# A fused attention and gated-FFN layer: one Strassen product for the down projections of chunks 0 and 1

## The chip, the cores and the metric

One core of a Trainium2 chip (trn2) runs one kernel launch. The metric is device time in microseconds (us), the time of that core. The kernel before took 777.2 us as the median of 3 runs (776.82 to 777.21).

## What is computed

Two layers in a row on 2048 positions of width 1024, in bf16: a pre-norm attention with a dilated window of 8 keys, and a pre-norm feed-forward part in which gate and up are multiplied without an activation.

```python
qkv = layernorm(x) @ wqkv                       # D = 1024, 32 heads of 32
logits[s, w] = q[s] . k[s - 2*w] * 32**-0.5     # w = 0..7, -1e9 where s - 2*w < 0
o = softmax(logits) @ v[s - 2*w]
h = x + o @ wo
n = layernorm(h)
out = h + ((n @ w_gate) * (n @ w_up)) @ w_down  # F = 3584
```

## The kernel before

The 2048 positions are worked in four chunks of 512 (TC). The width lies in eight blocks of 128 (KO), the hidden width F in 28 blocks of 128 (NF), or 14 pairs of blocks (NP). `tc.manual_schedule()` means that every engine runs its instructions in the order in which the Python code records them; nothing reorders them later.

Stages, in the order of TensorE:

- Query, key and value of all chunks (`qkv`, matmuls in `mm_group`, L409). ScalarE copies each result out of PSUM (L324) and SyncE's queue writes it to DRAM; GpSimd's queue reads it back in the layout of the attention (`load_qk`, `load_v`).
- Attention (`attention`, L444) runs on VectorE alone. It is a generator. First come the logits (L451 to L461), then the softmax, then eight weighted value products and their sums (L494, L499, L502, L504). At its end GpSimd's queue writes `oD` to DRAM (`od`, L506) and reads it back transposed as `oT`, in four parts (L509).
- The output projection of chunks 0 and 1 with the second layernorm (`wo_ln2`, L519): 64 matmuls (L532) in eight groups, VectorE's add of the residual (L534), the statistics (L181), the root on ScalarE (L185, L186), the normalised rows on VectorE (L190), and four transposing DMAs on SyncE's queue (L526), which together give `lnT`.
- Gate and up of chunks 0 and 1 (`ffn1`, L602): 448 matmuls a chunk, ScalarE copies (L611, L616), VectorE's product (L617), with ScalarE's sums of absolute values (`Scale.add`, L560) for the scales of the fp16 stages.
- The down projection of chunk 0 (`ffn2`, L640): 224 matmuls (L646), four results at a time. It stands between `wo_ln2(1)` and `ffn1(1)` (L777 to L825).
- The down projection of chunk 1 by Strassen's scheme within the chunk: its rows are split in two halves of 256 and its hidden blocks in even and odd ones. Seven products (`dprod`, L805) of 28 matmuls each take the place of 224. The operands are sums and differences in fp16, made by VectorE (L800, L929, L954, L958, L988); scaled copies come from ScalarE (L786) and VectorE (L788). The output projections of chunks 2 and 3 (`wo_adds`, L846; L934 and L969) stand between these products.
- Gate, up and down of chunks 2 and 3 together, by Strassen's scheme over both chunks (`pair_block`, L703, and `dprod`).

The order of VectorE's work around the change comes from `Background` (L37). Foreground code calls `bg.step(us)` after a group of matmuls; this adds that many microseconds (times `rate`) to a credit, and while the credit is positive the next step of a waiting generator, as a rule the attention, is recorded. `bg.spend(us)` takes VectorE's foreground work off the credit. `bg.finish(g)` records all that is left of a generator at that place. Thus the place of each attention operation in VectorE's list is fixed when the code is built.

Weights come through one list, `stream` (L130 to L156); `pump` (L161) issues the next load on SyncE's queue while fewer than seven tiles of `wstream` are in use, and `retire` (L173) gives tiles back. PSUM has eight banks, all under one tag.

Of the kernel before, what the change touches and what calls it, by code (L numbers as in the profile page):

```python
# [8 lines left out]
BF = mybir.dt.bfloat16  # L9
# [69 lines left out]
def kernel(  # L79
# [41 lines left out]

    bg = Background()
# [13 lines left out]
    def stream_wd(c, hf):  # L136
        for b in range(4):
            stream.append((("wd", c, hf, b), wd_v[:, bass.ts(b, 7), bass.ts(hf, 512)], 7))

    NH = NF // 4  # L140
    for c in range(2):
        stream_wo(c)
        if c > 0:
            stream_wd(0, 0)
            stream_wd(0, 1)
        for b in range(7):
            stream.append((("wg", c, b), wg_v[:, :, bass.ts(b, 512)], KO))
            stream.append((("wu", c, b), wu_v[:, :, bass.ts(b, 512)], KO))
    def stream_down(name, e, hf, halves):
        for a in halves:  # L150
            stream.append((("dn", name, a), wd_e[e][:, bass.ts(a, 7), bass.ts(hf, 512)], 7))

    stream_down("21", 1, 0, (0, 1))
    stream_down("11", 0, 0, (0, 1))
    stream_wo(2)
    stream_down("12", 0, 1, (0,))  # L156
# [286 lines left out]

    def attention(c):  # L444
        qD, kD = qkv_in["q", c], qkv_in["k", c]
        lg = att.tile([128, W, SUB], F32, tag="lg", name=f"lg{c}")
        for wp in range(W // 2):
# [14 lines left out]
            yield 1.0  # L462
        if c == 0:
            nc.vector.tensor_tensor(lg[0:32, :, 0:16], lg[0:32, :, 0:16], mask[:], ALU.add)
# [54 lines left out]
    def wo_ln2(c):  # L519
# [8 lines left out]
        for t in range(4):  # L528
            for hf in range(2):
# [5 lines left out]
                if hf == 1:  # L535
                    stats(hs[t], mv4, t)
                    rstd_of(mv4, rs4, t, t + 1)
                    bg.spend(1.5)
                elif t > 0:
                    norm(t - 1)  # L540
                    bg.spend(0.55)
                bg.spend(0.7)
                bg.step(GROUP_US)
# [38 lines left out]
    scale_gu, scale_d, scale_h = Scale("gu", 56), Scale("d", 56), Scale("h", 56)  # L582
    scale_h1 = Scale("h1", 28)

    def abs_sum(c, b, j):
        wt = wts["wg" if c == 0 else "wu", c, b]
        junk = lnp.tile([128, 2, 512], BF, tag="ln", name=f"junk{c}_{b}_{j}")
        scale_gu.add(28 * c + 4 * b + j, wt[:, bass.ts(j, 2), :], junk[:])

    def abs_sum_down(hf, b, j):  # L590
        junk = lnp.tile([128, 512], BF, tag="ln", name=f"junkd{hf}_{b}_{j}")
        scale_d.add(28 * hf + 7 * b + j, wts["wd", 0, hf, b][:, j, :], junk[:])
# [5 lines left out]
    def abs_sum_h1(f, ht):  # L598
        junk = lnp.tile([128, TC], BF, tag="ln", name=f"junke{f}")
        scale_h1.add(f, ht[:], junk[:])  # L600

    def ffn1(c, lnT, at={}):  # L602
        hT = []
        for b in range(7):
            if b == 5 and c + 1 < NCH:
                hss[c + 1] = load_x(c + 1, "h", nc.sync)
            for j in range(4):
                pg = psum.tile([128, TC], F32, tag="mm", name=f"pg{c}_{b}_{j}")
                mm_group(pg, wts["wg", c, b], j, lnT)
                gs = t1k.tile([128, TC], BF, tag="t1k", name=f"gs{c}_{b}_{j}")  # L610
                nc.scalar.copy(gs[:], pg[:])  # L611
                bg.step(GROUP_US)
                pu = psum.tile([128, TC], F32, tag="mm", name=f"pu{c}_{b}_{j}")
                mm_group(pu, wts["wu", c, b], j, lnT)
                us = t1k.tile([128, TC], BF, tag="t1k", name=f"us{c}_{b}_{j}")
                nc.scalar.copy(us[:], pu[:])  # L616
                nc.vector.tensor_tensor(gs[:], gs[:], us[:], ALU.mult)  # L617
                abs_sum(c, b, j)
                bg.spend(0.45)
                bg.step(GROUP_US)  # L620
                hT.append(gs)
                if (b, j) in at:
                    at[b, j]()
                f = len(hT) - 3
                if c == 1 and f >= 0:
                    abs_sum_h1(f, hT[f])
            retire(2)
            if b in at:
                at[b]()
        if c == 1:  # L630
            for f in range(NF - 2, NF):
                abs_sum_h1(f, hT[f])
        return hT

    def ffn2_store(c, t, hf, acc, hs, lo=0, n=512):
        cols = bass.ds(hf * 512 + lo, n)
        nc.vector.tensor_tensor(hs[t][:, cols], acc[:], hs[t][:, cols], ALU.add)
        nc.sync.dma_start(outf[bass.ds(c * TC + t * 128, 128), cols], hs[t][:, cols])

    def ffn2(c, hf, hT, hs, between={}):  # L640
        acc = [psum.tile([128, 512], F32, tag="mm", name=f"acc{c}_{hf}_{t}") for t in range(4)]
        for b in range(4):
            for j in range(7):
                f = b * 7 + j
                for t in range(4):
                    nc.tensor.matmul(acc[t][:], lhsT=hT[f][:, bass.ts(t, 128)],  # L646
                                     rhs=wts["wd", c, hf, b][:, j, :],
                                     start=(f == 0), stop=(f == NF - 1))
                if c == 0:
                    abs_sum_down(hf, b, j)  # L650
                bg.step(0.86)
            retire()
            if b in between:
                between[b]()
        for t in range(4):
            ffn2_store(c, t, hf, acc[t], hs)
            bg.spend(0.7)


# [104 lines left out]
    pump(pair_at)  # L764
    qkv(2, range(6))
    start_attention(2)
    hss[0] = load_x(0, "h", nc.sync)
    qkv(3, range(4), last=True)
    bg.finish(atts[0])
# [4 lines left out]
    lnT2, hs = nxt  # L774
    hT = ffn1(0, lnT2)
    bg.finish(atts[1])
    nxt = wo_ln2(1)  # L777
    for hf in range(2):
        ffn2(0, hf, hT, hs)
    lnT2, hs = nxt  # L780
# [37 lines left out]
    dn = {}  # L818

    def first_blocks():  # L820
        dn["11"] = [wts["dn", "11", a] for a in range(2)]
        dn["21"] = [wts["dn", "21", a] for a in range(2)]
        conv_down(dn["11"])

    hT = ffn1(1, lnT2, {0: scale_d.rows, 2: scale_d.total, (6, 1): first_blocks})  # L825
    hs1 = hs
    E1 = {"11": [t[:, 0:256] for t in hT[0::2]], "21": [t[:, 256:512] for t in hT[0::2]],
          "12": [t[:, 0:256] for t in hT[1::2]], "22": [t[:, 256:512] for t in hT[1::2]]}
    EF = {k: [f16(a) for a in E1[k]] for k in E1}
    conv_down(dn["21"], nc.scalar)  # L830
    scale_gu.rows()
    scale_h1.rows()
    bg.finish(atts[2])
    ex = [psum.tile([128, TC], F32, tag="mm", name=f"ex{q}") for q in range(2)]
    ey = [psum.tile([128, TC], F32, tag="mm", name=f"ey{q}") for q in range(2)]
    for q in range(2):
        dprod(ex[q], q, E1["11"], fcells(dn["11"]), True)
        bg.step(3.0)

    h3 = att.tile([128, 4, D], BF, tag="qD", name="h3")  # L840
    nc.sync.dma_start(h3[:], x[bass.ts(3, TC), :].rearrange("(t p) d -> p t d", p=128))
    hss[3] = [h3[:, t, :] for t in range(4)]
    ln2 = {c: ln_tiles(f"2_{c}") for c in (2, 3)}
    nbs = {}

# [40 lines left out]
    def ln_rows(c, t, lnT):  # L886
        rs4 = ln2[c][1]
        ln = lnp.tile([128, D], BF, tag="ln", name=f"lnr{c}_{t}")
        nc.scalar.activation(ln[:], hss[c][t][:], ACTF.Identity, bias=nbs[c][:, t:t + 1], scale=rs4[:, t:t + 1])
        nc.sync.dma_start_transpose(lnT[:, :, bass.ts(t, 128)], ln[:])  # L890

    def scales():
        scale_h1.total(ey[1])
        inv1 = const.tile([128, 1], F32, name="inv_h1d")
        nc.vector.tensor_tensor(inv1[:], scale_h1.inv, scale_d.inv, ALU.mult)
        dn["inv"] = inv1[:]
        for q in range(2):
            nc.scalar.activation(ey[q][:], ex[q][:], ACTF.Copy, scale=scale_h1.s)
        for k in range(NP):
            to_f16(f16(hT[2 * k][:]), hT[2 * k][:], scale_h1.s, nc.scalar)  # L900

    def second_blocks():
        bg.finish(atts[3])
        dn["px"] = att.tile([128, 2 * KO, TC], BF, tag="prod", name="prodx")
        dn["kx"] = att.tile([128, KO, TC], BF, tag="kD", name="kx")
        dn["vx"] = att.tile([128, KO, TC], BF, tag="vD", name="vx")
        dn["ox"] = att.tile([128, KO, TC], BF, tag="oD", name="ox")
        dn["lx"] = lnTp.tile([128, KO, TC], BF, tag="lnT", name="lx")
        dn["12"] = [wts["dn", "12", 0], dn["px"][:, 0:KO, :]]
        dn["22"] = [dn["ox"], dn["lx"]]  # L910
        nc.sync.dma_start(dn["12"][1][:, 0:NH, :], wd_e[0][:, bass.ts(1, NH), bass.ts(1, 512)])
        load_down(dn["22"], 1, 1)
        conv_down(dn["22"], nc.scalar)
# [76 lines left out]
    for t in range(4):  # L990
        ln_rows(3, t, l3)
# [166 lines left out]
```

## Time and profile before

| | |
|---|---|
| median of 3 runs | 777.2 us |
| the profiled execution: its time | 777.01 us |
| its span | 775.2 us |
| TensorE busy | 769.3 us (99%) |
| VectorE busy | 605.3 us (78%) |
| ScalarE busy | 484.0 us |
| DMA moved | 134.38 MB |
| granted TensorE clock | 1.0 |

The span is from the first to the last instruction that the profiler shows; the 1.8 us around it belong to the run's time. PE is TensorE, PEld its weight loads, DVE VectorE, ACT ScalarE, POOL GpSimd, SP SyncE. "L532" is line 532 of the kernel. A row of the timeline gives start, length, engine, line, operation, output and inputs, shape, and in brackets the time that the engine had been idle and what ended it. Matmuls overlap: one of 128x512 is shown with 379 ns, but the next begins after 216.

TensorE's stages in this profile: attention inputs until 163.4 us, `wo_ln2(0)` from 163.4, the rest of query, key and value from 177.2, `ffn1(0)` from 191.0, `wo_ln2(1)` from 287.7, `ffn2(0)` from 301.5, `ffn1(1)` from 349.9, the Strassen products of chunk 1 with the projections of chunks 2 and 3 from 446.6, the pair blocks from 516.8.

### The profile page before, as it was taken

What the parts mean: (1) busy time and instruction counts of PE and PEld (TensorE: products, weight loads), DVE (VectorE), ACT (ScalarE), POOL (GpSimd) and SP (SyncE); (2) the same over time, 40 slices, a digit from 0 to 9 for tenths busy, and PEclk for the clock granted to TensorE, in tenths of its full rate; (3) what the DMA queues carried; (4) which work ended last, traced back from release to release, by engine and by line L of the source; (5) the groups of instructions that cost most, each with busy time, mean ns of one, the idle gap of its engine ahead of it and who ended that gap; (6) DMA issues with size and microseconds to landing.
All of it is one profiled execution on the core that took longest, in us unless ns stands there. A gap on an engine that the chain in (4) does not pass through costs nothing.

```text
span 775.2 us, 10420 instructions
## 1 busy us (share of the span) xinstructions
PE 769.3 (99%) x3691; PEld 353.5 (46%) x3691; DVE 605.3 (78%) x766; ACT 484.0 (62%) x1040; POOL 142.1 (18%) x152
## 2 busy tenths in 40 slices
PE   8999999999999999999999999999999999999998
PEld 6444444444444444444444444444444444444444
DVE  5639999999999989999979859985553444578863
ACT  4639564322866662965777899746677776788240
POOL 0000000200002000011000001008778687600000
PEclk9999999999999999999999999999999999999999
DMA  8998896997947964978445592644332423740001
GB/s 278 265 260 199 157 230 151 299 271 224 310 133 236 308 235 125 288 257 277 142 143 192 182 299 68 157 98 114 109 95 69 109 59 106 240 140 28 0 28 55
DMA packets 183716, 134.38 MB, mean 173 GB/s; under 512 B 81264, under 2 KB 176496, under 8 KB 181616
## 3 DMA queue, kind: packets, MB, share of 16 engines
q1 hardware_dynamic: 176912, 110.12, 50.9%
q0 software_dynamic: 3584, 22.02, 8.9%
q10 hardware_dynamic: 3168, 1.57, 0.8%
q8 instruction: 29, 0.48, 0.3%
q14 instruction: 23, 0.19, 0.1%
HBM read 104.86 MB, written 22.02 MB: 164 GB/s over the span
## 4 chain that ended last, share of the span: by engine, by line
PE 93%; DVE 3%; DMA 2%; ACT 1%; issue 0%; ACTq 0%; DVEq 0%
PE ps L411 20%; PE pg L411 12%; PE pu L411 12%; PE dx L807 6%; PE pz L700 6%; PE acc L646 6%; PE py L700 6%; PE px L700 6%; PE wo L532 4%; PE wo L852 4%; PE pv L700 3%; PE dy L807 3%; PE ex L807 2%; DMA lnT<-lnr 1%; DMA w_qkv<-in_A_wqkv_dram 1%; PE ps L372 1%
## 5 line engine op out<-in xcount | busy, mean ns | idle before, releaser
L411 PE MATMUL ps<-lnT,w_qkv 128*128 128x512 bf16 x736 | 159.5, 379 | 0.0
L411 PEld LDWEIGHTS <-w_qkv 128*128 128x128 bf16 x736 | 71.9, 98 | 86.2
L411 PE MATMUL pu<-lnT,w_wu 128*128 128x512 bf16 x448 | 105.8, 379 | 0.0
L411 PE MATMUL pg<-lnT,w_wg 128*128 128x512 bf16 x448 | 105.8, 379 | 0.0
L324 ACT CAST sg<-ps 128x512 bf16<-128x512 f32 x96 | 55.2, 585 | 52.3 <-PE ps L411 49.2
L451 DVE TENSOR_TENSOR prod<-qD,kD 128x4096 bf16<-128x4096 bf16 x32 | 72.4, 2285 | 12.8 <-DMA kD<-kd 12.7
L494 DVE TENSOR_TENSOR pv<-vD,at 128x4096 bf16<-128x4096 bf16 x32 | 72.5, 2285 | 0.3
L700 PEld LDWEIGHTS <-sw 128*128 128x128 f16 x448 | 43.8, 98 | 53.8 <-issue 1.2
L411 PEld LDWEIGHTS <-w_wu 128*128 128x128 bf16 x448 | 43.8, 98 | 52.9
L411 PEld LDWEIGHTS <-w_wg 128*128 128x128 bf16 x448 | 43.7, 98 | 52.8
L616 ACT CAST us<-pu 128x512 bf16<-128x512 f32 x56 | 33.0, 590 | 43.0 <-PE pu L411 41.8
L700 PE MATMUL px<-lnT,ws 128*128 128x512 bf16 x224 | 55.2, 379 | 0.0
L700 PEld LDWEIGHTS <-ws 128*128 128x128 f16 x336 | 32.9, 98 | 39.7
L506 POOL DMA_DIRECT2D od<-oD x4 | 2.2, 542 | 264.3 <-DVE oD L504 264.3
L646 PE MATMUL acc<-w_wd,gs 128*128 128x512 bf16 x224 | 48.5, 379 | 0.0
L681 POOL TENSOR_TENSOR sw<-ws 128x512 f16<-128x512 f16 x26 | 30.0, 1152 | 85.1 <-PE py L700 77.8
L611 ACT CAST gs<-pg 128x512 bf16<-128x512 f32 x56 | 32.6, 583 | 12.9 <-PE pg L411 10.6
L453 DVE TENSOR_TENSOR prod<-prod 128x4096 bf16<-128x4096 bf16 x16 | 36.6, 2289 | 0.4
L560 ACT ACTIVATE junkd<-w_wd 128x512 bf16<-128x512 bf16 x56 | 34.3, 613 | 0.0
L646 PEld LDWEIGHTS <-gs 128*128 128x128 bf16 x224 | 21.9, 98 | 26.4
L617 DVE TENSOR_TENSOR gs<-gs,us 128x512 bf16<-128x512 bf16 x56 | 23.5, 419 | 12.5 <-ACT us L616 12.5
L185 ACT ACTIVATE rs<-mv,eps 128x1 f32<-128x1 f32 (+1 forms) x21 | 6.2, 297 | 42.0 <-DVE mv L182 36.6
(321 smaller groups left out, 1391.5 us busy)
## 6 DMA issues: line engine op xcount, KB each, us to landing
w_wg<-in_B_w_gate_dram SPq DMA_DIRECT2D x14, 1024.0 KB, 6.7
w_wu<-in_B_w_up_dram SPq DMA_DIRECT2D x14, 1024.0 KB, 5.4
w_wd<-in_B_w_down_dram SPq DMA_DIRECT2D x8, 896.0 KB, 6.2
w_pair<-in_B_w_gate_dram SPq DMA_DIRECT2D x14, 512.0 KB, 4.0
w_pair<-in_B_w_up_dram SPq DMA_DIRECT2D x14, 512.0 KB, 5.2
w_wo<-in_A_wo_dram SPq DMA_DIRECT2D x6, 1024.0 KB, 6.2
w_qkv<-in_A_wqkv_dram SPq DMA_DIRECT2D x5, 1024.0 KB, 11.0
kd<-sg SPq DMA_DIRECT2D x32, 144.0 KB, 3.3
```

The costliest lines, as they stand in the source:

```text
L324: nc.scalar.copy(sg[:, HB:HB + TC], ps[:])
L411: nc.tensor.matmul(ps[:], lhsT=wt[:, ko, bass.ts(j, 128)], rhs=rhs[:, ko, :], start=(ko == 0), stop=(ko == KO - 1))
L451: nc.vector.tensor_tensor(prod[:, j], qD[:], kD[:, :, o:o + SUB], ALU.mult)
L453: nc.vector.tensor_tensor(prod[:, :, 0:16], prod[:, :, 0:16], prod[:, :, 16:32], ALU.add)
L494: nc.vector.tensor_tensor(pv[:, j], vD[:, :, o:o + SUB], at[:, w, None, :].to_broadcast((128, DH, SUB)), ALU.mult)
L532: nc.tensor.matmul(ps[:], lhsT=oTs[c][:, kk, t, :], rhs=wts["wo", c, hf][:, kk, :], start=(kk == 0), stop=(kk == KO - 1))
L560: nc.scalar.activation(junk, src, ACTF.Abs, accum_out=self.l1[:, k:k + 1])
L611: nc.scalar.copy(gs[:], pg[:])
L616: nc.scalar.copy(us[:], pu[:])
L646: nc.tensor.matmul(acc[t][:], lhsT=hT[f][:, bass.ts(t, 128)], rhs=wts["wd", c, hf, b][:, j, :], start=(f == 0), stop=(f == NF - 1))
L700: nc.tensor.matmul(ps[:], lhsT=lhs[:, ko, :], rhs=rhs[:, ko, :], start=(fresh and ko == 0), stop=(ko == 3), skip_group_check=not fresh)
L807: nc.tensor.matmul(ps[:, bass.ds(lo, n)], lhsT=lhs[k][:, bass.ts(q, 128)], rhs=rhs[k][:, bass.ds(lo, n)], start=(fresh and k == 0), stop=( ...
```

## The change

The down projection of chunk 0 leaves its place. Chunks 0 and 1 become the two halves of one Strassen product: seven products of 56 matmuls each, after `ffn1` of chunk 1. So:

- `ffn1_second` (chunk 1) follows `wo_ln2(1)` at once.
- Chunk 0's 28 gated blocks stay in their tiles (`t1k`, 30 buffers). Chunk 1's are made in a ring of two `lnT` tiles, written to DRAM (`hd1`) in pairs of blocks, and read back as `a21` and `a22`, the latter twice.
- The product of gate and up is recorded one group of matmuls later than the copy of up. The abs-sums are coarser (1024 and 2048 columns at once).
- The down weights' scale is summed from eight blocks loaded for that alone, four of them during `qkv(2)` ahead of the first projection's weights, four during `ffn1_second`.
- The residual rows that are still wanted go to DRAM (`hsd`) after each projection and come back later.
- The attention of chunk 3 is recorded through its logits and softmax maximum before the products begin (`while 3 not in scored`); what is left of it goes by credit, and the remainder is recorded at `bg.finish(atts[3])`, ahead of `wo_adds(3)`.
- Some of chunk 2's and 3's gated blocks get other homes (`rooms`).

The core of the diff:

```diff
     hss[0] = load_x(0, "h", nc.sync)
     qkv(3, range(4), last=True)
+    bg.finish(sums)
     bg.finish(atts[0])
     bg.rate = 0.98
     nxt = wo_ln2(0)
     qkv(3, range(4, 6), last=True)
     start_attention(3)
-    lnT2, hs = nxt
-    hT = ffn1(0, lnT2)
+    hT0 = ffn1_first(nxt[0])
     bg.finish(atts[1])
+    sums = abs_gen((4, 5, 6, 7))
+    bg.add(sums, bg.now, first=True)
     nxt = wo_ln2(1)
-    for hf in range(2):
-        ffn2(0, hf, hT, hs)
-    lnT2, hs = nxt
+    ffn1_second(nxt[0], {4: lambda: bg.finish(sums)})
...
-    hT = ffn1(1, lnT2, {0: scale_d.rows, 2: scale_d.total, (6, 1): first_blocks})
...
+    while 3 not in scored:
+        next(atts[3])
...
+    b12 = halves(((att, "qD"), (att, "kD")), "b12")
+    load_down(b12, 0, 1)
+    a21 = halves(((lnTp, "lnT"), (lnTp, "lnT")), "a21")
+    a22 = halves(((lnTp, "lnT"), (wpool, "w")), "a22")
...
+    load_h1(a21, 0)
+    load_h1(a22, 1)
...
+    for q in range(4):
+        dprod(xs[q], q, A11, cells_of(b11, NH), True)
+        if q == 1:
+            scale_d.total(ys[2])
+            scale_h1.total(ys[3])
...
+            bg.spend(2.0)
         bg.step(3.0)
...
+    sh1, sd1 = scale_h1.s, scale_d.s
+    for q in range(4):
+        nc.vector.tensor_scalar(ys[q][:], xs[q][:], sd1, sh1, ALU.mult, ALU.mult)
+        bg.spend(0.75)
+    for t, n in ((a21[0], 8), (a22[0], 8), (a21[1], 6), (a22[1], 6)):
+        to_f16(f16(t[:, 0:n, :]), t[:, 0:n, :], sh1, nc.scalar)
+    for q in range(4):
+        dprod(xs[q], q, A12, cells_of(b21, NH), False)
+        put(0, q, 0, hs0[q][:, 0:512], xs[q], 1.0, hs0[q][:, 0:512])
+        bg.spend(0.75)
+        t = (b11 + b12)[q]
+        to_f16(f16(t[:, 0:NH, :]), t[:, 0:NH, :], sd1)
+        bg.spend(1.1)
+        bg.step(3.0)
...
+    wo_adds(2, {0: in_turn(lambda: s1_half(0), lambda: conv_a(A11, F11, 0, 5)),
+                1: in_turn(lambda: s1_half(1), b22_homes, lambda: conv_a(A11, F11, 5, 10)),
+                2: in_turn(lambda: t_half(b11, b12, b11, 0), lambda: conv_a(A11, F11, 10, 14)),
+                3: lambda: t_half(b11, b12, b11, 1), 4: lambda: conv_a(A12, F12, 0, 5),
+                5: lambda: conv_a(A12, F12, 5, 10), 6: lambda: conv_a(A12, F12, 10, 14)})
...
+        s_sums(F11, FS1, F11, ALU.subtract, (0, 4, 8, 14)[q], (4, 8, 14, 14)[q])
+        if q >= 2:
+            t_half(t2, b22, b11, q - 2)
+        bg.step(3.0)
...
+    for q in range(4):
+        dprod(ys[q], q, F12, fcells(b22), False)
+        rest = restf[:, bass.ts(q % 2, TC)]
+        nc.vector.tensor_tensor(rest, p5t[q][:], hsr0[:, q, :], ALU.add)
+        put(0, q, 1, hsr0[:, q, :], ys[q], inv1, rest)
+        bg.spend(1.4)
+        if q < 2:
+            t_half(b12, b22, b12, q)
+        bg.step(3.0)
+    bg.finish(atts[3])
+    scale_gu.rows()
+    a22 = halves(((att, "vD"), (att, "oD")), "a22r")
+    load_h1(a22, 1)
...
     retire(2)
+    hs3 = hss[3]
     load_pair(0)
...
+    for q in range(4):
+        dprod(zs[q], q, F11, fcells(b12), False)
...
+        put(1, q, 1, hsr1[:, q, 512:1024], zs[q], inv1, p5t[q][:])
+        if q < 2:
+            t_half(t4, b21, t2, q)
+        ln_rows(3, q, l3)
...
+    for q in range(4):
+        dprod(zs[q], q, F22, fcells(t4), False)
+        put(1, q, 0, hsr1[:, q, 0:512], zs[q], inv1, hsr1[:, q, 0:512])
```

`put` is VectorE's scaled add out of PSUM with its store to the output; `t_half` is `sub` on half a weight part; `s_sums` is one VectorE operation for each of the given blocks. `ffn1_second` is:

```diff
+    def ffn1_second(lnT, at):
+        ring = [lnTp.tile([128, KO, TC], BF, tag="lnT", name=f"ring{i}") for i in range(2)]
+        junk = ring[1][:, 4:8, :]
+        late = []
+
+        def finish():
+            i, g, u = late.pop(0)
+            nc.vector.tensor_tensor(g, g, u, ALU.mult)
+            bg.spend(0.75)
+            scale_h1.add(NF + i, g, junk[:, 0:2, :])
+            nc.sync.dma_start(hd1[:, bass.ts(i, 2), :], g)
+
+        for b in range(7):
+            if b == 5:
+                hss[2] = load_x(2, "h", nc.sync)
+            for j in range(4):
+                i, k = divmod(4 * b + j, 2)
+                part = ring[i % 3 // 2][:, bass.ts(i % 3 % 2, 4), :]
+                g, u = part[:, 0:2, :], part[:, 2:4, :]
+                for what, dst in (("wg", g), ("wu", u)):
+                    ps = psum.tile([128, TC], F32, tag="mm", name=f"p{what}1_{b}_{j}")
+                    mm_group(ps, wts[what, 1, b], j, lnT)
+                    nc.scalar.copy(dst[:, k, :], ps[:])
+                    if what == "wg" and late:
+                        finish()
+                    if what == "wu":
+                        if k:
+                            late.append((i, g, u))
+                        if j % 2:
+                            abs_sum("wu", b, j // 2, junk)
+                    bg.step(GROUP_US)
```

## The prediction

> **What bounds the kernel now.** I read the page's busy lines and slices first, then TensorE in order of time, then the engines that feed it around the change.
>
> ```profile
> span 775.2 us, 10420 instructions
> ...
> PE 769.3 (99%) x3691; PEld 353.5 (46%) x3691; DVE 605.3 (78%) x766; ACT 484.0 (62%) x1040; POOL 142.1 (18%) x152
> ...
> PE   8999999999999999999999999999999999999998
> PEld 6444444444444444444444444444444444444444
> DVE  5639999999999989999979859985553444578863
> ```
>
> TensorE works 769.3 of 775.2 us; by windows it rests 2.2 us in the first 60, 0.6 between 517 and 560 and 2.9 at the end, behind the last matmul. So only matmuls taken away can gain, and every new wait of TensorE is a loss. VectorE is nearly full between slices 4 and 18: it has little room to come early.
>
> ```profile
> 1.20 5.05 PE L318 MATMUL warm_ps<-warm 128*128 128x512 bf16 x13 [1.20 <-DVE warm L304]
> ...
> 287.72 13.98 PE L532 MATMUL wo<-w_wo,oT 128*128 128x512 bf16 x64
> 301.53 48.51 PE L646 MATMUL acc<-w_wd,gs 128*128 128x512 bf16 x224
> 349.88 1.89 PE L411 MATMUL pg<-lnT,w_wg 128*128 128x512 bf16 x8
> ```
>
> Chunk 1's output projection (L532) ends at 301.5. Then 48.3 us of chunk 0's down projection run before the gate matmuls of chunk 1 want chunk 1's normalised, transposed rows. A matmul costs 48.35/224 = 0.216 us.
>
> ```profile
> 304.21 0.68 DVE L534 TENSOR_TENSOR h<-wo,h 128x512 bf16<-128x512 f32 x1
> ...
> 306.93 0.55 DVE L190 TENSOR_SCALAR ln<-h,mv,rs 128x1024 bf16<-128x1024 bf16 x1 [0.60 <-ACT rs L186]
> ```
> ```profile
> 297.97 10.77 SPq L526 DMA_TRANSPOSE lnT<-ln  x4
> ```
> ```profile
> DMA to landing us min/median/max: 3.0/3.1/3.2
> ```
>
> These are VectorE, the SyncE queue, and the landing of the four transposes: the last norm ends at 307.5, its transpose is issued there and lands near 310.6. That is 9 us after L532 ends, and today nobody sees it.
>
> ```profile
> 337.19 2.29 DVE L502 TENSOR_TENSOR pv<-pv 128x4096 bf16<-128x4096 bf16 x1
> 339.51 2.29 DVE L504 TENSOR_TENSOR oD<-oD,pv 128x4096 bf16<-128x4096 bf16 x1
> ```
> ```profile
> 342.10 0.54 POOL L506 DMA_DIRECT2D od<-oD  x1 [65.79 <-DVE oD L504]
> 347.42 3.54 POOL L509 DMA_DIRECT2D oT<-od  x4 [4.78 <-DMA od<-oD]
> ...
> 440.19 0.56 POOL L506 DMA_DIRECT2D od<-oD  x1 [88.68 <-DVE oD L504]
> ```
>
> An attention result goes to DRAM and back. VectorE's last add for chunk 2 ends at 341.8, the way back is issued at 347.4, and such a load lands in a median 4.8 us: 10.4 us from VectorE to the projection's input. Chunk 3's result leaves at 440.2, while its projection starts at 478.8.
>
> **What the skill says.** "Perfetto Trace Analysis", Tensor Engine Instruction: VectorE and ScalarE are strictly first in, first out, and TensorE can only pull weight loads ahead. So the order of instructions decides, and I read it for both kernels; the rows above, each behind its engine's own, agree. "TensorE: Matmul & The Clock Gate", Back-to-back issue gap: N/2.4 + 2.5 ns, 216 ns for 512 columns; the trace gives 216. The same page, What's actually happening: after an idle window of some 3.4 us the array runs at half clock until about 3.4 us of work are done. The trace bears out a price: the 13 first matmuls took 5.05 us where 13 x 0.216 + 0.16 (the longer last record) is 2.97, so 2.1 us lost. No longer rest is in this trace.
>
> **The change part by part.**
>
> *Matmuls.* Before: 224 plain ones for chunk 0 and 7 products of 28 for chunk 1, 420. After: 7 products of 56, 392. 28 x 0.216 = 6.05 us off the path. The two small waits before the first pair block (0.41 and 0.22 us) may go: -0.6.
>
> *(a) Chunk 1's rows.* The change puts chunk 1's gate matmuls straight behind its output projection. The order of after shows their first weight load waiting on the four transposes; 48 us of cover is gone. Behind the waiting load stands all of TensorE's list, and ScalarE and VectorE, which read its banks, have only attention and abs-sums left meanwhile. VectorE's list up to there is that of before, but for gated products shifted by a group, so the rows come at 310.6 + 0.1 against 301.5: 9.2 us. Were VectorE not late, add, statistics, root, norm and transpose (0.7 + 1.5 + 0.6 + 0.5 + 3.1) would still be 6.4; with ScalarE or the new stores of residual rows (four 256 KB writes in the same queue) in the way I allow 11. I take 9.2.
>
> *(b) Scales.* After ffn1 of chunk 1 (its end is P) ScalarE still has a copy (0.6), the sum of a 128x2048 weight part (no row; 1.07 us for 1024 and 3.69 for a 4096 pass give about 2.0) and the last row sum (1.1): P + 3.9. VectorE then has the two reductions (P + 4.4), a queued oD add (P + 6.7), eleven small scale operations of 0.15 to 0.19 (P + 8.4), pv's two multiplies and add (6.75, P + 15.2), and only then the first scaled copy of a partial sum. That copy has no row (PSUM to PSUM, two scalars): L534 with PSUM took 0.67, ScalarE's L898 0.62; 0.7, at most 1.25. The third product accumulates in that bank, so TensorE, done with the first product at P + 12.4, waits until P + 15.9: 3.5 us (2 to 5).
>
> *(c) Around the projection of chunk 2.* Between adds of 0.68 VectorE must do an oD add (2.3), the two halves of S1 (2.3, 1.7) and two differences of 2.0. With four banks free, the eighth group waits some 0.8 us for an add, the next product 0.9. ScalarE's conversions (A21 and A22, 13 us, then 28 of 0.64, then b22, 2 x 3.2) end about when t2 is wanted: 0 to 2, I take 1. Sum 2.7.
>
> *(d) Chunk 3's attention.* In VectorE's order six operations of it (L502, L504, two L494, L502, L504 of before) stand behind the last store of the fourth product, which waits for TensorE; the next thing on TensorE is chunk 3's projection. From the end of that product: 0.95 for the store, 2.3 + 2.3 + 4.5 + 2.3 + 2.3 = 13.7, then 10.4 to DRAM and back, 0.2 of handover: 25.2 us, nothing else in TensorE's queue. The oT loads landed in 3.5 to 9.7, so 23.5 to 30. Today this lead is 38 us.
>
> *(e)* During that projection VectorE has eight adds, two conversions (2.2), 14 subtractions of 0.34 (estimate: start to start of such rows) and four statistics; the second half of F11 is ready some 2 us after TensorE asks: 2.0 (0 to 3).
>
> *Re-warming.* (a) and (d) are far beyond 3.4 us: 2 x 2.1 = 4.2; (b) is at the edge, 0 to 2, taken as 0.
>
> *Moved at no cost.* Gated products a group later, ring writes and abs-sums: ScalarE's load stays (sums 138 us both ways by the durations above), and eight banks let TensorE run 12 us ahead; if a block of sums holds ScalarE longer, the excess is added. The early down blocks (4 x 0.9 MB) stand in SyncE's queue before the first projection weights; these are issued near 134 and wanted at 163, and a weight load lands in about 6 (DMA issues). The DRAM way of chunk 1's rows (3.7 MB out, 5.5 MB in), residual rows (1.6 out and in) and two more down blocks (1.8) make 14 MB more than 134; the A21 loads stand in SyncE's queue behind the last ring write, and have 15 us until S1. GpSimd's list keeps its order. The normalised rows of chunks 2 and 3 move into the last two products, on ScalarE (8 x 1.24) and in SyncE's queue (eight transposes of 3.3 to landing): by my count the last lands 17 us behind chunk 3's projection and VectorE's four sums for the pair blocks (4.9) end 25 us behind it, with the pair block's second product wanted at 28. That cover is 3 us thick; what is missing would be added.
>
> Sum: -6.05 - 0.6 + 9.2 + 3.5 + 2.7 + 25.2 + 2.0 + 4.2 = +40.1 us. The profiled run was 777.0 (span 775.2, 1.8 around it): 817.1 us. The median of the runs, 777.2, is 0.2 above it, which is within their spread.
>
> **Rivals.** *Only the matmuls count* (not slower): if VectorE finished chunk 3's attention 25 us earlier and the transposes were covered, 777.0 - 6.7 = 770.3. The saving decides while all new waits stay below 6.7 us. For it speaks that TensorE has no wait today in all these stages; against it that the order fixes (d). 3%. *The attention's tail is hidden*: VectorE's six operations done before TensorE's fourth product ends, so that (d) and its warm-up go: 817.1 - 27.3 = 789.8. The 38 us of lead today speak for it; six operations behind a store that waits for TensorE against. 7%. *The DRAM way is late too*: 5.5 MB of down blocks and A parts in one queue need 20 us at the 275 GB/s that the windows show between 310.7 and 350; at half that rate S1 is 10 to 15 us late, and TensorE stands there also: 830. 13%. That the change does not what it says: the order has 28 matmuls fewer and the seven products; excluded.
>
> **How the numbers follow.** 77% for 817 with its own range 806 to 826 from the bounds of (a) to (e) and warm-up. The range of 80% reaches towards the late rival: 804 to 830. This measurement can tell about 0.2% from no change. Faster 3%, within 0.2% 1%, slower 96%.
>
> **What would show it.** After: an idle gap of 9 us before chunk 1's first gate matmul, released by the transposes; 25 us before chunk 3's projection, released by oT; 3 to 4 us before the third product, released by VectorE; the first 13 or so matmuls after the long gaps at double spacing. It is wrong if VectorE does the six operations before that product's stores, or if the gap at oT is under 20 us.

## The result, and the profile after

The changed kernel takes 839.6 us in the median (838.91 to 842.83, 4 runs) against 777.2 before (776.82 to 777.27): a ratio of 1.081, 95% interval 1.078 to 1.084. The forecast was 817.1, with a range of 804 to 830. The sign and five of the waits were forecast; a sixth place, which the forecast took to cost nothing, was not. The profiled execution took 839.5 us, its span is 837.7.

The page of the changed kernel, lines as they were shown of before:

```profile
span 837.7 us, 10321 instructions
...
PE 777.8 (93%) x3663; PEld 353.5 (42%) x3663; DVE 616.7 (74%) x736; ACT 504.1 (60%) x972; POOL 142.0 (17%) x152
...
PE   9999988599999997999998994399999999999998
...
DVE  5549999929999989599986969298544444458943
...
PEclk9999998799999998999999997599999999999999
```

TensorE is busy longer than before (777.8 us with 28 matmuls fewer, since part of them ran at a lower clock) and rests 60 us. A slice is 20.9 us. Counted from 1, those at 16, 22 and 25 to 26 are (a), (b) and (d) of the forecast; the hole at 6 to 8 was not forecast, and the clock fell there too. TensorE's waits of the same kernel, by what ended them:

```profile
PE wo L934 <- DMA oT<-od: 26.3, 1, 26.3
PE ps L421 <- ACT halo L339: 13.5, 2, 10.3
PE pwg L421 <- DMA lnT<-ln: 6.2, 1, 6.2
PE ps L421 <- ACT sg L334: 4.0, 2, 2.5
PE ex L853 <- DVE ey L906: 3.0, 1, 3.0
```

Columns: who waited for what, us in all, times, the longest. The first, third and fifth are (d), (a) and (b). The second and fourth, 17.5 us together, are matmuls of query, key and value that wait for ScalarE to empty a PSUM bank. They lie before the first projection, in TensorE's list in order of time:

```profile
111.21 10.52 PE L421 MATMUL ps<-lnT,w_qkv 128*128 128x512 bf16 x48 [1.49 <-ACT sg L334]
124.20 10.48 PE L421 MATMUL ps<-lnT,w_qkv 128*128 128x512 bf16 x40 [2.47 <-ACT sg L334]
137.93 10.48 PE L421 MATMUL ps<-lnT,w_qkv 128*128 128x512 bf16 x40 [3.25 <-ACT halo L339]
158.71 28.01 PE L421 MATMUL ps<-lnT,w_qkv 128*128 128x512 bf16 x120 [10.29 <-ACT halo L339]
186.56 13.76 PE L545 MATMUL wo<-w_wo,oT 128*128 128x512 bf16 x63
```

The projection of chunk 0 starts at 186.56; before, at 163.40. That is 23.2 us: 17.5 of waits, and 5.7 that are nearly all matmuls at the lower clock after them (40 matmuls take 40 x 0.216 + 0.16 = 8.8 at full clock, not 10.48; the last three groups of this stage lost 1.7, 1.7 and 1.9). What ScalarE did meanwhile:

```profile
102.83 0.59 ACT L334 CAST sg<-ps 128x512 bf16<-128x512 f32 x1
109.54 1.06 ACT L577 ACTIVATE junkd<-w_wd 128x1024 bf16<-128x1024 bf16 x1 [6.12 <-DMA w_wd<-in_B_w_down_dram]
...
122.53 1.06 ACT L577 ACTIVATE junkd<-w_wd 128x1024 bf16<-128x1024 bf16 x1 [6.25 <-DMA w_wd<-in_B_w_down_dram]
...
135.95 1.06 ACT L577 ACTIVATE junkd<-w_wd 128x1024 bf16<-128x1024 bf16 x1 [5.95 <-DMA w_wd<-in_B_w_down_dram]
...
156.73 1.06 ACT L577 ACTIVATE junkd<-w_wd 128x1024 bf16<-128x1024 bf16 x1 [12.99 <-DMA w_wd<-in_B_w_down_dram]
```

ScalarE stands four times, 31.3 us in all, at the first sum over a down block that is still on its way. Its copies of PSUM stand behind that sum, and TensorE behind the copies. SyncE's queue shows when those loads were issued:

```profile
103.17 0.95 SPq L177 DMA_DIRECT2D w_wd<-in_B_w_down_dram  x1
...
116.78 0.54 SPq L177 DMA_DIRECT2D w_wd<-in_B_w_down_dram  x1
...
130.28 0.46 SPq L177 DMA_DIRECT2D w_wd<-in_B_w_down_dram  x1
...
144.01 1.91 SPq L177 DMA_DIRECT2D w_wd<-in_B_w_down_dram  x1
```

Only one tile is free for these blocks (six hold the query, key and value weights), so a block is issued only when the sums of the one before it are done. A block thus takes its way (6 us, the fourth 12.7), four sums, and the copies between them: 13.6 us from issue to issue. The fourth was on its way while GpSimd's queue fetched `oT` and `vD` (issued from 142.75 to 146.28); that this is why it took 12.7 is not shown. In ScalarE's list 6, 5 and 5 PSUM copies stand between the first sums of consecutive blocks, and five groups of matmuls are 5 x 1.73 = 8.65 us. At 13.6 us for 8.65 the lead of eight banks is soon gone.

### The profile page after: what moved, and what is told of

It is laid out like the page before. It is cut to its first block, busy times and chain, and to the rows that moved or that the text cites. A ratio compares the mean times of both kernels' runs of the same rounds, so it can differ in the third digit from the quotient of the medians.

```text
span 837.7 us, 10321 instructions
## 1 busy us (share of the span) xinstructions
PE 777.8 (93%) x3663; PEld 353.5 (42%) x3663; DVE 616.7 (74%) x736; ACT 504.1 (60%) x972; POOL 142.0 (17%) x152
## 5 line engine op out<-in xcount | busy, mean ns | idle before, releaser
L421 PE MATMUL ps<-lnT,w_qkv 128*128 128x512 bf16 x736 | 165.5, 388 | 17.5 <-ACT halo L339 13.5
L421 PE MATMUL pwg<-lnT,w_wg 128*128 128x512 bf16 x224 | 54.6, 388 | 6.2 <-DMA lnT<-ln 6.2
L934 PE MATMUL wo<-w_wo,oT 128*128 128x512 bf16 x128 | 30.1, 395 | 26.5 <-DMA oT<-od 26.3
L421 PE MATMUL pwu<-lnT,w_wu 128*128 128x512 bf16 x224 | 54.1, 385 | 0.0
L421 PE MATMUL pg<-lnT,w_wg 128*128 128x512 bf16 x224 | 52.9, 379 | 0.0
L421 PE MATMUL pu<-lnT,w_wu 128*128 128x512 bf16 x224 | 52.9, 379 | 0.0
L577 ACT ACTIVATE junkd<-w_wd 128x1024 bf16<-128x1024 bf16 (+1 forms) x32 | 31.3, 978 | 31.3 <-DMA w_wd<-in_B_w_down_dram 31.3
L853 PEld LDWEIGHTS <-gs 128*128 128x128 f16 (+1 forms) x280 | 27.6, 99 | 39.2 <-issue 5.4
L760 ACT COPY py<-px 128x512 f32<-128x512 f32 x28 | 16.0, 570 | 28.9 <-PE px L743 28.9
L934 PEld LDWEIGHTS <-oT 128*128 128x128 bf16 x128 | 12.9, 101 | 43.3 <-DMA oT<-od 26.8
```

Of the source, the lines that this page charges most:

```text
L421: nc.tensor.matmul(ps[:], lhsT=wt[:, ko, bass.ts(j, 128)], rhs=rhs[:, ko, :], start=(ko == 0), stop=(ko == KO - 1))
L577: nc.scalar.activation(junk, src, ACTF.Abs, accum_out=self.l1[:, k:k + 1])
L760: nc.scalar.copy(yb[i][:], xb[i][:])
L853: nc.tensor.matmul(ps[:, bass.ds(lo, n)], lhsT=lhs[k][:, bass.ts(q, 128)], rhs=rhs[k][:, bass.ds(lo, n)], start=(fresh and k == 0), stop=( ...
L934: nc.tensor.matmul(ps[:], lhsT=oTs[c][:, kk, t, :], rhs=wts["wo", 2, hf][:, kk, :], start=(kk == 0), stop=(kk == KO - 1))
```

## The experiments

Theory A: the early sums, recorded as soon as the load is issued, cost 23 us by ScalarE's place in the order; rivals are the 3.7 MB themselves and the other new parts. Theory B: the rest are the waits (a), (b) and (d) as forecast, with matmuls at a lower clock after each. Times of the kernel before in these three series were 777.0, 777.3 and 777.1 us. The changed kernel's variants scatter by several us between runs, so each edit is read from its trace first.

**Sums later.** In `abs_gen`:

```diff
+            yield "later", 5 * GROUP_US
             for k in range(4):
                 abs_sum_down(i, k)
```

> From the changed kernel: the sums over each early down block are recorded five groups of matmuls (8.7 us) after the block's load instead of at once, so that ScalarE finds the block landed. Theory (ScalarE, in order, stood 31.3 us at the sums for loads just issued, and the copies of the query/key/value banks stood behind it): ScalarE's wait on w_wd falls from 31.3 to under 8 us, TensorE's waits on ScalarE's copies before the first projection from 17.5 to under 3, the clock there is 1.0, wo_ln2(1) starts near 289 instead of 310.9. Part of it comes back: without the long rest of TensorE VectorE no longer catches up, so the wait of chunk 1's gate matmuls on the transposes goes from 6.2 to about 9. Time 839.6 - 22 + 3 = about 820. Rival (the 3.7 MB themselves are too much for the queue or for the DMA engines at this place): TensorE's waits stay above 10 us, time above 830.

Measured: 820.8 us (818.05 to 823.56), ratio 1.056 (1.053 to 1.059), 18.8 under the changed kernel's median. ScalarE waits 5.4 us for the blocks, TensorE not at all for its copies. TensorE in order of time:

```profile
99.78 63.40 PE L421 MATMUL ps<-lnT,w_qkv 128*128 128x512 bf16 x287
163.02 1.89 PE L545 MATMUL wo<-w_wo,oT 128*128 128x512 bf16 x8
165.84 12.26 PE L545 MATMUL wo<-w_wo,oT 128*128 128x512 bf16 x55 [0.93 <-DMA w_wo<-in_A_wo_dram]
```

The projection starts at 163.0, as before the change, and the span of this trace is 22.4 us shorter. The weights of the projection, which stand behind the blocks in SyncE's queue, now come 0.9 us late. The expected return did not come: the wait ahead of chunk 1's gate matmuls stayed at 6.2 us (this trace puts it down to a VectorE operation of the same moment), so VectorE had not been helped by TensorE's rest.

**No early blocks.** The stream and the sums without blocks 0 to 3:

```diff
-    for i in range(4):
-        stream_wd(i)
...
-    sums = abs_gen(range(4))
-    bg.add(sums, bg.now, first=True)
+    nc.vector.memset(scale_d.l1[:], 0.0)
...
-    bg.finish(sums)
```

> From the changed kernel: the four early down blocks are neither loaded nor summed (the down scale then comes from the other four blocks only; this part of the computation is left out). Theory: the same as with later sums, since the place of the sums and not the load is what costs: about 818 to 820, waits on ScalarE's copies before the first projection 0, and a wait of about 9 us at the transposes of chunk 1. Rival (the loads cost by their bytes or their place in SyncE's queue): this run is over 8 us faster than the one with later sums.

Measured: 816.6 us (814.49 to 823.38), ratio 1.052 (1.048 to 1.057). That is 4 us under the run before, within the scatter of both; the projection starts at 163.28, and its weights are not late. So it is the place of the sums that cost 23 us. The loads are not quite free once the sums are moved: in four of the five runs with later sums the projection's weights came late, by 0.9 us above and by 2.8, 4.4 and 4.1 in runs further down. This run is the change without the unforeseen part, and its time is near that of the forecast (817.1).

**The early blocks alone, in the kernel before.** The same four loads ahead of the first projection's weights, with sums recorded in the same way:

```diff
+    for i in range(4):
+        stream.append((("we", i), wd_v[:, bass.ts(i, 7), 0:512], 7))
...
+    sums = early_gen()
+    bg.add(sums, bg.now, first=True)
     qkv(2, range(6))
...
+    bg.finish(sums)
```

> The kernel before, with one part of the change alone: the four early down blocks in the stream ahead of the first projection's weights and their sums on ScalarE, recorded as soon as each load is issued (their values are used for nothing). Theory: ScalarE stands some 30 us at loads on the way, TensorE waits 17 to 21 us for its copies and runs part of that stage at a lower clock, the first projection starts at 186 to 189 instead of 163.4, and all later stages keep their lengths: 777 + 23 to 26 = 800 to 803. Rival (it is the chunk 1 rows, the ring or some other part of the change that holds up the early stage): within 3 us of 777.

Measured: 802.7 us (802.34 to 803.55), ratio 1.033 (1.032 to 1.035). TensorE:

```profile
118.86 11.92 PE L413 MATMUL ps<-lnT,w_qkv 128*128 128x512 bf16 x48 [8.88 <-ACT sg L326]
131.83 9.00 PE L413 MATMUL ps<-lnT,w_qkv 128*128 128x512 bf16 x40 [1.05 <-ACT sg L326]
147.43 11.26 PE L413 MATMUL ps<-lnT,w_qkv 128*128 128x512 bf16 x40 [6.60 <-ACT halo L331]
162.08 27.75 PE L413 MATMUL ps<-lnT,w_qkv 128*128 128x512 bf16 x120 [3.39 <-ACT halo L331]
189.66 10.52 PE L534 MATMUL wo<-w_wo,oT 128*128 128x512 bf16 x48
```

19.9 us of waits and 6.3 of slower matmuls, and all later stages together as long as before. The waits are split otherwise than in the changed kernel: SyncE's queue came to the first block at 110.57 here and at 103.17 there, so ScalarE stood 15.8 us at the first sum. With this, theory A is shown from both sides: taken out of the changed kernel and put alone into the other.

**Attention earlier.** One line ahead of `ffn1_second`:

```diff
+    bg.rate = 1.07
     ffn1_second(nxt[0], {4: lambda: bg.finish(sums)})
```

> From the changed kernel: the rate of the background work is 1.07 instead of 0.98 from the gate and up matmuls of chunk 1 on, which puts five attention operations of VectorE more ahead of the end of that stage and the last sum of chunk 3's attention ahead of the fourth product's adds. Theory (VectorE had 13 us idle in that stage and 8 in the second half of the first product, and the projection of chunk 3 waited only because six operations were recorded behind the last store): the wait at oT falls from 26.3 to 0 to 2, the first matmuls after it run at full clock (2 us), new waits of the products on VectorE are up to 3 us: 839.6 - 26 - 2 + 1.5 = about 813. Rival (VectorE has no room, its work only moves: waits before the third product and in the S1 product grow by as much): above 828.

Measured: 819.9 us (816.49 to 824.85), ratio 1.056 (1.051 to 1.061). The wait at `oT` is gone, with the slow group behind it: the cause of (d) is shown. But a part came back as waits on VectorE:

```profile
PE ey L587 <- DVE rowbd L582: 3.3, 1, 3.3
PE ex L854 <- DVE ey L907: 3.1, 1, 3.1
PE ez L854 <- DVE gs L1010: 2.0, 1, 2.0
...
PE ey L587 <- DVE rowbh L582: 1.0, 1, 1.0
```

The two first products together took 37.0 us instead of 29.3, the ones after 2.4 more, against 28.5 gained at `oT`. (The early stage was 2.6 us longer in this trace.) VectorE had less room than its idle time said. A likely reason, not tried apart, is that the idle pieces lie between operations that wait for TensorE and ScalarE, so that an added operation makes the row sums late.

**Layernorm covered.** The projection of chunk 1 ahead of the last block of `ffn1_first`:

```diff
+            if b == 6:
+                bg.finish(atts[1])
+                nxt1.append(wo_ln2(1))
...
     for b in range(7):
+        if b == 6:
+            stream_wo(1)
         stream_gu(0, b)
-    stream_wo(1)
```

> From the changed kernel: the output projection of chunk 1 with its layernorm stands ahead of the last block of gate and up of chunk 0 (64 matmuls, 13.8 us) instead of behind it, its weights a block earlier in the stream. Theory: the 13.8 us cover the 6.2 us until the transposes land, and the two slow groups after it (3.57 and 3.07 us instead of 1.89 and 1.73) run at full clock: 839.6 - 6.2 - 3.0 = about 830.4. Rival (the rows are late because VectorE is late, so that the wait only moves by the order of the list, or moves to the attention of chunk 3): within 3 us of 839.6.

Measured: 834.1 us (832.36 to 836.05), ratio 1.073 (1.071 to 1.075). The wait and the two slow groups are gone: gate and up of chunk 1 take 96.7 us, not 99.5. 3.8 us come back in the first two products (the wait for the scaled copies is 4.8, not 3.0), which fits a VectorE that no longer has those 6 us to run ahead in; that alone was not tried.

**Scaled copies on ScalarE.**

```diff
-        nc.vector.tensor_scalar(ys[q][:], xs[q][:], sd1, sh1, ALU.mult, ALU.mult)
-        bg.spend(0.75)
+        nc.scalar.activation(ys[q][:], xs[q][:], ACTF.Copy, scale=s1d[:])
```

> From the changed kernel: the four scaled copies of partial sums (ys from xs) are made by ScalarE with the product of the two scales, not by VectorE behind three attention operations. Theory: the third product no longer waits (3.0 us) and runs at full clock (1.6 us lost there). VectorE gets 3 us, so two more attention operations come ahead of the last store of the fourth product, and the wait at oT falls from 26.3 to about 21.7. Time 839.6 - 4.6 - 4.6 = about 830.4. Rival (ScalarE's 13 us of conversions behind these copies make S1 late): new waits before the S1 product, time 835 or more.

Measured: 839.5 us (834.55 to 839.53), ratio 1.078 (1.075 to 1.081): no gain that can be told. The trace has what was expected of (b) (no wait, the two products 24.6 us instead of 29.3) and of (d) (21.9 instead of 26.3), and the rival too. TensorE's list:

```profile
486.07 1.67 PE L853 MATMUL ey<-t,gs 128*128 128x512 f16 x7 [0.87 <-DVE t L846]
489.81 12.42 PE L853 MATMUL ey<-t,gs 128*128 128x512 f16 x49 [2.07 <-DVE t L846]
```

The product with `t2` waits, because VectorE waited 4.6 us for `b22` (0.7 in the changed kernel), which ScalarE now converts later in relation to the products. This product takes 3.9 us more, the one ahead of it 1.0 more; the early stage happened to be 2.4 longer. The wait moved from one engine to the other.

**The gap filled.** 110 matmuls whose result nobody reads, ahead of the projection of chunk 3:

```diff
+    fill = psum.tile([128, TC], F32, tag="mm", name="fill")
+    for i in range(110):
+        nc.tensor.matmul(fill[:], lhsT=ones[:], rhs=A12[13], start=True, stop=True)
     scale_gu.rows()
```

and, in a second run, `range(121)`.

> From the changed kernel: 110 matmuls whose result nobody reads (128x512, 23.8 us) stand ahead of the projection of chunk 3, in the time in which TensorE waits 26.3 us for oT. They take nothing away of what it waits for. Theory (after such a wait the array runs at a lower clock, 3.5 us lost in the projection of chunk 3): the wait for oT falls to about 2, the first group takes 1.9 instead of 3.6 us, and the end comes 3.5 us earlier: 836.1. Rival (the first group is slow because of its operands' way and not because of the rest): 839.6, or later where the fill holds up the chain.

> From the changed kernel: as the filled gap, with 121 matmuls (26.1 us) instead of 110, so that TensorE rests under 1 us and not 3.05 us before the projection of chunk 3. In the run with 110 the first group took 3.54 us after a rest of 3.05. Theory (a rest of 3 us is already enough for the lower clock, one of up to 2.5 us is not: groups after rests of 1.4 and 2.5 us in the early stage showed no loss): the first group takes 1.9 us, the end comes 1.9 us earlier, 837.7. Rival (the slow first group has another cause): 3.5 us again, 839.6.

Measured with 110: 841.2 us (835.95 to 842.99), ratio 1.081 (1.077 to 1.085). The group behind the filling was slow as ever, though TensorE had rested only 3.05 us:

```profile
510.64 23.90 PE L1054 MATMUL fill<-gs,ones 128*128 128x512 bf16 x107
537.59 3.54 PE L934 MATMUL wo<-w_wo,oT 128*128 128x512 bf16 x8 [3.05 <-DMA oT<-od]
```

With 121: 838.2 us (830.47 to 840.12), ratio 1.076 (1.070 to 1.081):

```profile
511.72 26.28 PE L1054 MATMUL fill<-gs,ones 128*128 128x512 bf16 x121
538.57 1.90 PE L934 MATMUL wo<-w_wo,oT 128*128 128x512 bf16 x8 [0.57 <-DMA oT<-od]
```

The slow group is due to the rest. From its start to the product with `ez` this projection takes 14.04 us here and 15.99 in the changed kernel: the price is 2.0 us, not the 3.5 of the first expectation. That is below the scatter of the times, so the trace alone says it.

**All four together.** The four diffs above, at rate 1.07; then the same with the totals of the scales a quarter of a product later:

```diff
-        if q == 1:
+        if q == 2:
             scale_d.total(ys[2])
...
-        bg.step(3.0)
+        if q > 1:
+            bg.step(6.0)
```

> The four edits together: sums of the early blocks later, projection of chunk 1 a block earlier, rate 1.07 in the gate and up stage of chunk 1, the scaled copies on ScalarE. If the terms simply add: 839.6 - 23 - 9 - 4.6 - 29.8 = 773 to 777, below the kernel before only by about the 6 us of matmuls that were saved. Theory of VectorE (its list is full from 110 us to the end of gate and up of chunk 1, and every long wait of TensorE so far let it catch up; with the waits gone its lateness comes back as waits at the row sums, before S1 and before the fourth product): 10 to 20 us of new waits on VectorE, 785 to 795.

> As the run with all four edits, and the totals of the two scales stand one quarter of a product later on TensorE, with no attention operation recorded between the row sums and the scales. Theory of VectorE: the waits at the row sums (a few us where both stand in one product) go, those before S1 and later stay; 3 to 5 us faster than the run with all four: 780 to 790. If the terms simply add, the same as that run, 773 to 777.

Measured: 793.3 us (790.54 to 795.22), ratio 1.021 (1.018 to 1.024), and 793.6 (791.48 to 797.27), ratio 1.021 (1.018 to 1.025). The terms do not add to 775; the theory of VectorE's full list gave 785 to 795. The two times can't be told apart. What TensorE waits for in the first of them:

```profile
PE wo L546 <- DMA w_wo<-in_A_wo_dram: 2.8, 2, 1.6
PE ey L588 <- DVE rowbd L583: 2.7, 1, 2.7
PE ez L859 <- DVE gs L1016: 2.1, 1, 2.1
PE ey L859 <- DVE t L852: 1.8, 1, 1.8
PE pwu L422 <- DMA w_wu<-in_B_w_up_dram: 1.7, 1, 1.7
PE wo L941 <- DVE h L943: 1.5, 3, 0.6
...
PE ey L588 <- DVE rowbh L583: 1.0, 1, 1.0
```

Nothing is over 3 us, yet together they are more than the 6.05 us of matmuls saved. Of the 14.6 us of waits around the change 9.7 are for VectorE, just under the 10 to 20 of the theory; 4.9 are for loads, which it did not name. So the time lies in its range in part for another reason. The second kernel has the wait at the row sums down to 1.2 us and instead 4.8 at `t2` (1.8 in the first): the waits move along VectorE's list and do not go.

**GpSimd for VectorE.** On top of all four, with three early blocks, the second part of S1 and 20 differences of gated blocks on GpSimd, at two rates:

```diff
-        nc.vector.tensor_tensor(f16(s1[i][:, 0:n, :]), f16(a21[i][:, 0:n, :]), f16(a22[i][:, 0:n, :]), ALU.add)
+        (nc.gpsimd if i else nc.vector).tensor_tensor(f16(s1[i][:, 0:n, :]), f16(a21[i][:, 0:n, :]), f16(a22[i][:, 0:n, :]), ALU.add)
...
+            s_sums(F11, FS1, F11, ALU.subtract, 8, 14, nc.gpsimd)
...
+            s_sums(F12, F12, F11, ALU.subtract, 7, 14, nc.gpsimd)
```

> The four edits together with rate 1.03, only three early down blocks (the fourth is loaded with the later ones), and GpSimd instead of VectorE for the second part of S1 (3072 columns) and for 20 of the 42 differences of gated blocks (1.15 us each on GpSimd by the weight sums of the pair blocks). VectorE is relieved of some 8.5 us between the first product and the second half of F11. Theory of VectorE (its full list is what is left of the loss): the waits on VectorE in the products fall from 15 to about 6 us, the wait for the first projection's weights goes: 793.3 - 3 - 9 = about 781. Rival (GpSimd's operations take longer than their price beside VectorE's, or slow VectorE's): 790 or more, with waits on GpSimd's blocks before the third and fourth products.

> As the run with GpSimd at rate 1.03, but rate 1.05: about one attention operation more ahead of the end of gate and up of chunk 1 and the last sum of chunk 3's attention a product earlier. Theory of VectorE: within 3 us of the run at 1.03, since what comes earlier is paid at the row sums. If the place of the last sum decides: 3 or more us faster.

Measured: 793.4 us (790.68 to 795.54), ratio 1.021 (1.018 to 1.023), and 799.2 (797.7 to 799.35), ratio 1.028 (1.027 to 1.030). The rival of the first came true; both expectations of the second missed. VectorE and GpSimd at rate 1.03:

```profile
435.45 6.63 DVE L852 TENSOR_TENSOR w_dn<-b,w_dn 128x3584 f16<-128x3584 f16 x1
```

```profile
432.94 7.26 POOL L986 TENSOR_TENSOR s<-a,a 128x3072 f16<-128x3072 f16 x1 [80.71 <-ACT a L838]
440.27 10.52 POOL L1016 TENSOR_TENSOR gs<-s,gs 128x512 f16<-128x512 f16 x6
455.10 20.97 POOL L1016 TENSOR_TENSOR gs<-gs,gs 128x512 f16<-128x512 f16 x7 [4.31 <-ACT ep L1024]
```

A difference of VectorE that takes 2.02 us alone took 6.63 and ended at 442.1 beside GpSimd's sum, which ended at 440.2; TensorE waited 4.1 us for the add behind it. GpSimd's own took 10.52/6 = 1.75 and 20.97/7 = 3.0 us, for 1.15 in the pair stage. At rate 1.05 the row sums came late by 4.0 us and the add by 5.5. But the longer time does not come from there. The first projection, up to which both kernels record the same, started at 169.45 and not at 163.28: SyncE's queue came to the first early block 6.3 us later (108.90 against 102.56), and the projection's weights were 4.1 us late; why is open. Behind the start of that projection both take the same (627.6 and 627.1 us), as the theory of VectorE said. No version tried is faster than the kernel before.

## Why the forecast was wrong

Going by its own steps:

- *Matmuls.* Right: each product of 56 starts 12.08 or 12.09 us after the one before it where nothing waits.
- *(a)* forecast 9.2, measured 6.2. The low end, "were VectorE not late" (6.4), was the true case. VectorE's first add of this projection, before and after:

```profile
294.08 1.28 DVE L534 TENSOR_TENSOR h<-wo,h 128x512 bf16<-128x512 f32 x2
```
```profile
314.21 1.28 DVE L547 TENSOR_TENSOR h<-wo,h 128x512 bf16<-128x512 f32 x2
```

It starts 6.4 us behind TensorE's first matmul before the change (287.72) and 3.3 after it (310.88); 3.3 also with later sums, 4.3 without the early blocks. The forecast took VectorE's list to be that of before but for the shift of the gated products by a group. That shift is what it missed: with it the four small operations of the softmax run ahead of that first matmul and not behind it, and the last add follows its matmul at once.

- *(b)* forecast 3.5, measured 3.0, on the path named. (The product that waits, called the third in the forecast, is the second in TensorE's order.)
- *(c)* forecast 2.7, measured 0.9.
- *(d)* forecast 25.2, measured 26.3. VectorE's six operations stand behind the store, as forecast; the higher rate shows that they are the cause. The store, and the last of the six:

```profile
511.31 0.75 DVE L701 SCALAR_TENSOR_TENSOR hsr<-ey,inv_h1d,hsr 128x512 bf16<-128x512 f32 x1 [0.93 <-PE ey L853]
...
523.47 2.29 DVE L517 TENSOR_TENSOR oD<-oD,pv 128x4096 bf16<-128x4096 bf16 x1
```

- *(e)* forecast 2.0, measured 0.8 + 0.4.
- *Re-warming* forecast 4.2 for (a) and (d), measured 2.8 and 2.0, and 1.6 behind (b), which had been taken as 0.
- *Moved at no cost* is the step that failed: 0 forecast, 23.2 measured. It asked of the early down blocks only whether they delay the projection weights behind them in SyncE's queue (it had these issued near 134; they were issued at 165.58 and 174.15). It counted the sums as load on ScalarE ("ScalarE's load stays") and had the lead of TensorE, 12 us, as cover. It did not ask when ScalarE comes to the first sum of a block. Most numbers were at hand: a weight load lands in about 6 us, one tile is free, four sums of about 1 us lie among five groups of 1.73. Per block that makes 13.6 us on ScalarE for 8.65 on TensorE; the 12.7 us of the fourth load was not at hand. ScalarE stood 31.3 us in all. An estimate from this and the lead of 12 is 19.3 us for TensorE; its waits were 17.5.

By these numbers the rest of the sum holds: -6.05 - 0.3 + 6.2 + 3.0 + 0.9 + 26.3 + 1.2 + 6.4 = 37.7, with the early stage 60.9 of the 62.5 us by which the span grew; what is left is two matmuls for the totals (0.4) and some 0.16 at each of seven waits, which the lists count from the modelled end of the last matmul and not from when the next could have begun. The -0.3 is the small wait before the first pair block, 0.3 where 0.6 was before and 0 was forecast. The forecast without its wrong step, 817.1, stands beside 816.6 for the run without early blocks. Part of that is luck: the terms were off by -3.0 (a), -0.5 (b), -1.8 (c), +1.1 (d), -0.8 (e), +2.2 (re-warming) and +0.3, which happen to nearly cancel with the 1.6 left out, and the executions of that run lie between 814.5 and 823.4. The rival of the late DRAM way, which gave 830, did not come. ScalarE waits 10.8 us for the first rows read back for `a21`, but TensorE does not: ahead of the product with S1 it waits 0.65 us for an add. "The attention's tail is hidden" was made by hand with the higher rate, and gave 20 us, not 27.

## What to carry to other kernels

A load whose result an in-order engine reads must be recorded as far ahead of its reader as it takes to land; ask it of each new load, and ask it of the reader's queue, not only of the queue that issues the load. Count how often a lead (here eight banks, 12 us) is drawn upon: with later sums one long wait of ScalarE was covered (5.7 us with all four edits, 10.3 with the totals later, none of it a wait of TensorE for its copies); four in a row, 31.3 us, were not. Where two engines are nearly full, a wait taken away can come back further down the other's list: terms of 23, 9, 5 and 28 us (65 in all), each of which went with its edit, gave 46 together.

## What was not expected of the hardware

*How short a rest makes TensorE slow.* The forecast put the edge at 3.4 us, after "TensorE: Matmul & The Clock Gate", What's actually happening. By that no shorter rest should do it, and here several did; the measurement decides. With all four edits a rest of 2.10 us was followed by a granted clock of 0.50 in the next 2 us and cost 0.9 (49 matmuls took 12.41 us, against 11.47 behind a rest of 2.02 at rate 1.07). One of 2.47 cost 1.7 (the second of the four above), one of 2.96 cost 1.6 (b), one of 3.05 cost 1.6 (the filled gap). Others cost at most 0.2: that of 2.02, one of 2.42 in the same run, one of 2.46 in the run with 110 matmuls. So the edge is not sharp in these runs: rests of 1.01, 1.49, 1.92 and 2.01 us cost at most 0.2, and from 2.1 to 2.5 some cost and some did not. Two rests of 0.87 and 2.07 with seven matmuls between (scaled copies on ScalarE) cost 1.7. A window that runs freely, of which the same section speaks, would give such an uncertain edge; the window itself is not seen here. The price does not follow the length of the rest: 6.2 us cost 2.8 (a), 10.29 cost 1.9, 26.3 cost 2.0 (d).

*GpSimd beside VectorE.* "SBUF — State Buffer", SBUF: two separate sides, calls the port pair that both use an exclusive lock, held for a whole instruction. The trace agrees with it: VectorE's 2.02 us difference took 6.63 and ended where GpSimd's end and its own time put it (440.2 + 2.0 for 442.1). At rate 1.05 VectorE's sum of S1, 2.28 us alone, took 8.09 and ended at 449.97, where GpSimd's end and its own time give 447.8 + 2.3. GpSimd's 1.15 us operations took 1.75 and 3.0 on average. So a price from a stage in which VectorE is half idle did not hold in one in which it is full.
